# The first load of queries and keys as one of 120 rows and one of 8

## The chip, the core and the metric

The kernel runs on one core of one Trainium2 chip. The metric is the device time of one execution in microseconds (us); the kernel's time is the median of several runs. A core has TensorE (PE; its weight loads are shown apart as PEld), VectorE (DVE), ScalarE (ACT), GpSimd (POOL) and SyncE (SP), each with its own instruction queue, and 16 DMA engines. SPq and ACTq in the rows are the parts of SyncE and ScalarE that issue transfers.

## What is computed

Attention with decay (no softmax) over 8 batches, 8 heads, 576 positions and 64 numbers per head, then a mixture of 8 experts that skips some tokens:

```python
scores = scale * np.matmul(q, k.transpose(0, 1, 3, 2))
Dmat = np.where(rel >= 0, gamma[:, None, None] ** rel[None, :, :], 0.0)
attn = np.matmul(scores * Dmat[None], v)
x = attn.transpose(0, 2, 1, 3).reshape(4608, 512)
do_compute = x @ w_skip > 0
e_idx = np.argmax(x[do_compute] @ w_gate, axis=1)
# for the tokens of expert e: y = gate_w * (relu(xc @ w1[e]) @ w2[e]); out = xc + y; the others: out = x
```

## The kernel before

The 4608 tokens are 36 tiles of 128. The first stage is the attention: for each tile g, SyncE loads a buffer `u` of four sections of 128 rows (partitions) in two halves. The first half (sections 0 and 1) holds queries and keys, 128 rows of 4 KB; the second (sections 2 and 3) holds values and keys in another layout. The second stage, from about 150 us, gathers the tokens of each expert and does the expert products with weights `w`. There are five `u` buffers, so that a load waits until the tile five before it has been used.

At the start the kernel issues, in this order: the decay table `tab_sb` on ScalarE's queue; on SyncE's queue the loads (0, 0), (1, 0), (0, 2), (2, 0), (1, 2), a growth table `gt_sb`, (3, 0), (2, 2), (3, 2), where (g, s) is tile g from section s on; and the router's weights `wg_sb`. Tile 4 and the later ones follow.

While the first load is under way, TensorE runs nine products on a cleared tile (`keep_up`, line 117), and a few more between the first tiles. What it does for tile g afterwards:

- `scores(g)` (line 572, into `psc` and `psq`) needs the first half. Each pair of products reads rows 0 to 63 and rows 64 to 127 of `u` in turn.
- `decay(g)`: VectorE multiplies the scores by masks (lines 587 and 590; the far part also by `dq_sb`, which VectorE makes of the decay table, line 545), and ScalarE copies the rest (line 594) back into `u`.
- `keys(g)` and `rows_of(g)`: GpSimd scales the keys `kn` (line 602) and the values `vs` (line 624) of the second half.
- `state(g)` (line 638), `second(g)` (line 663) and `values(g)` (line 687) are products that need those, and VectorE writes the tile's result (line 699).

The order on each engine comes from a scheduling layer that follows the program's order and the dependences. It gives the transfers of SyncE and ScalarE eight semaphores in rotation: a transfer waits until the one eight places before it has landed.

Of the kernel before, what the change touches and what calls it, by code (L numbers as in the profile page):

```python
# [11 lines left out]
F32 = mybir.dt.float32  # L12
# [10 lines left out]
NTOK, DM, NE, DF = B * S, H * D, 8, 1024  # L23
P = 128
# [3 lines left out]
NPR = H // 2  # L28
# [19 lines left out]
UBUFS = 5  # L48
# [2 lines left out]
AHEAD = 5  # L51
LEAD = 3
GLATE = 4
GROUPS = (8, 8, 8, 4, 4, 4)
KONE = 2
QD = 32
# [32 lines left out]
def kernel(  # L89
# [9 lines left out]
    nc = tc.nc  # L99
# [23 lines left out]
    trank = const.tile([P, NT], F32, tag="trank", name="trank")  # L123
    exs = [const.tile([P, max(GROUPS), NE + 1], F32, tag=f"ex{i}", name=f"ex{i}") for i in range(2)]
    ident = const.tile([P, P], F32, tag="ident", name="ident")
# [19 lines left out]

    cp = ps_m[:, SIDE : SIDE + max(GROUPS) * NCMP].rearrange("p (t k) -> p t k", k=NCMP)
    iota8 = const.tile([P, NE], F32, tag="iota8", name="iota8")
# [68 lines left out]

    starts = np.cumsum((0,) + GROUPS).tolist()

    def tile_numbers(t0, n):
        nc.vector.tensor_copy(cp[:, :n, 0], tidx[:, t0 : t0 + n])  # L220

    def route_b(ps, first, late, pin, n, t0, ex, mb):
# [17 lines left out]
        if first:  # L240
            nc.vector.tensor_copy(cp[:, :, 1], pidx[:, : max(GROUPS)])
            tile_numbers(t0, n)
# [21 lines left out]
        if t0 + n < NT:  # L264
            tile_numbers(t0 + n, GROUPS[starts.index(t0 + n)])

# [226 lines left out]
    with ExitStack() as actx:  # L493
        ac = actx.enter_context(tc.tile_pool(name="ac", bufs=1))
        ap = actx.enter_context(tc.tile_pool(name="ap", bufs=2))
# [14 lines left out]

        u_t = {}

        def load_half(g, s, after=None):
            if s == 0:
                u_t[g] = ap.tile([P, 4, NPR, P], F32, tag="u", name=f"u_{g}", bufs=UBUFS)
            n = 1 if s and g % NQ == HALF else 2
            half = nc.sync.dma_start(
                u_t[g][:, s : s + n].rearrange("p s a i -> p (s a i)"),
                qkv[g, s // 2, :, : n * DM],
            )  # L520
            if after is not None:
                tc.add_manual_dep(
                    half.ins,
                    after.name,
                    mybir.DependencyInfo(mybir.DependencyClass.Sync, mybir.DependencyReason.DATA),
                    reason="the second half begins behind a block of products",
                )

        def last_product():
            return next(i for i in reversed(nc.cur_bb.bb.instructions) if i.engine == mybir.EngineType.PE)  # L530

        nc.scalar.dma_start(tab_sb, tab)
        for g, s in ((0, 0), (1, 0), (0, 2), (2, 0), (1, 2), (3, 0), (2, 2), (3, 2)):
            load_half(g, s)
            if (g, s) == (1, 2):
                nc.sync.dma_start(gt_sb[:, 0], gtab.rearrange("p (a q) -> p a q", a=NPR))
# [94 lines left out]
        def state(g):  # L631

            i = g % NQ
            if i == HALF:
                return
            for a in range(NPR):
                for j in range(2):
                    nc.tensor.matmul(
                        ps_s[halves[j], i % 2, a, :],
                        kn_t[g][:, a, j * D : (j + 1) * D],  # L640
                        u_t[g][:, 2, a, j * D : (j + 1) * D],
                        start=i == 0 and a == 0,
                        stop=a == NPR - 1,
                        skip_group_check=True,
                    )
                yield
            if i == HALF - 1:
                st_t[g + 1] = ap.tile([P, NPR, D], F32, tag="sv", name=f"sv_{g}", bufs=1)
                nc.scalar.copy(st_t[g + 1], ps_s[:, 1])
                return  # L650
            to = joint(g + 2)
            for j in range(2):
                nc.scalar.copy(to[halves[j], j], ps_s[halves[j], i % 2])
# [19 lines left out]
        def in_turn(*products):  # L673

            products = list(products)
            while products:
                products = [p for p in products if next(p, p) is not p]
# [3 lines left out]
        def values(g):  # L681

            pxt = px_t[g]
            q = first(g)
            for a in range(NPR):
                for j in range(2):
                    nc.tensor.matmul(  # L687
                        pxt[halves[j], a, q],
                        vs_t[g][:, j, a, :],
                        u_t[g][:, j, a, q],  # L690
                        start=False,
                        stop=a == NPR - 1,
                        skip_group_check=True,
                    )
                yield
            b, o = divmod(g, NB)
            if o == 0:
                xt_t[b] = ap.tile([P, NPR, NB * P], F32, tag="xt", name=f"xt_{b}")
            nc.vector.tensor_tensor(xt_t[b][:, :, o * P : (o + 1) * P], pxt, gt_sb[:, g % NQ // 2], ALU.mult)
# [64 lines left out]
        def weights():  # L764
# [7 lines left out]
            while held and (held[0] < KFRONT or "first" in marks):  # L772
# [3 lines left out]
                tc.keep_in_program_order(nc.scalar.copy(hi, t))  # L776
                behind = ranked[-1] if len(ranked) == len(GROUPS) - 1 else None
                for m in range(2):
# [78 lines left out]
        for g in range(NT):  # L857
# [5 lines left out]
            in_turn(*products)  # L863
            if g == GLATE:
                load_half(g + UAHEAD - 1, 0, last_product())
            if g and g + UAHEAD - 1 < NT:
                load_half(g + UAHEAD - 1, 2, last_product())
# [17 lines left out]
            in_turn(state(g), *([values(last)] if last >= 0 else []))  # L885
            if g + 1 != GLATE and g + UAHEAD < NT:
                load_half(g + UAHEAD, 0)
# [4 lines left out]
        g = NT  # L892
# [521 lines left out]
```

## Time and profile before

| | us |
|---|---|
| median of 3 runs | 390.61 |
| lowest and highest run | 386.76, 394.09 |
| the profiled execution: its time | 390.34 |
| the profiled execution: its span | 388.6 |
| TensorE busy | 367.6 |
| VectorE busy | 276.0 |
| ScalarE busy | 181.7 |
| GpSimd busy | 152.5 |

The span is the time from the first to the last instruction of the profiled execution; its own time holds 1.7 us more. Busy times overlap between engines. A row of a timeline gives the start, the duration, the engine, the source line, the operation with the tile that it writes and those that it reads, how many instructions were merged, and in brackets how long the engine had been idle before and what ended that.

### The profile page before, as it was taken

What the parts mean: (1) busy time and instruction counts of PE and PEld (TensorE: products, weight loads), DVE (VectorE), ACT (ScalarE), POOL (GpSimd) and SP (SyncE); (2) the same over time, 40 slices, a digit from 0 to 9 for tenths busy, and PEclk for the clock granted to TensorE, in tenths of its full rate; (3) what the DMA queues carried; (4) which work ended last, traced back from release to release, by engine and by line L of the source; (5) the groups of instructions that cost most, each with busy time, mean ns of one, the idle gap of its engine ahead of it and who ended that gap; (6) DMA issues with size and microseconds to landing.
All of it is one profiled execution on the core that took longest, in us unless ns stands there. A gap on an engine that the chain in (4) does not pass through costs nothing. (4 is left out here: it accounts for less than half of the span.)

```text
span 388.6 us, 12328 instructions
## 1 busy us (share of the span) xinstructions
PE 367.6 (95%) x4886; PEld 334.5 (86%) x4886; DVE 276.0 (71%) x615; ACT 181.7 (47%) x369; POOL 152.5 (39%) x211
## 2 busy tenths in 40 slices
PE   7899998989999898999999999999999999999991
PEld 3678877777887776888899999999999999999991
DVE  3576677578579794877856767867878768687762
ACT  2464555355544576117445455445545545555311
POOL 5885855555475389260136000420322322002032
PEclk9999999999999999999999999999999999999997
DMA  8989997989999988257899768978899898776511
GB/s 305 404 281 375 394 351 270 347 299 341 320 359 331 313 319 260 63 128 252 261 317 262 264 212 276 327 228 303 275 278 329 249 336 313 233 253 228 142 68 61
DMA packets 49573, 106.15 MB, mean 273 GB/s; under 512 B 6102, under 2 KB 21206, under 8 KB 49511
## 3 DMA queue, kind: packets, MB, share of 16 engines
q1 hardware_dynamic: 40951, 85.81, 65.2%
q0 software_dynamic: 3232, 9.99, 7.9%
q10 hardware_dynamic: 5328, 9.52, 6.5%
q8 instruction: 40, 0.66, 0.7%
q14 instruction: 22, 0.18, 0.1%
HBM read 83.51 MB, written 22.28 MB: 272 GB/s over the span
## 5 line engine op out<-in xcount | busy, mean ns | idle before, releaser
L171 DVE TENSOR_TENSOR wlo_w<-w,whi_w 128x1024 fp32r<-128x1024 f32 x59 | 72.0, 1223 | 37.8 <-ACT whi_w L170 35.4
L170 ACT CAST whi_w<-w 128x1024 fp32r<-128x1024 f32 x59 | 61.7, 1050 | 33.1 <-PE py L465 32.4
L465 PE MATMUL py<-hlo,whi_w 128*128 128x336 f32 (+6 forms) x224 | 67.8, 303 | 0.0
L465 PE MATMUL ph<-xhi,wlo_w 128*128 128x336 f32 (+6 forms) x224 | 67.6, 302 | 0.0
L465 PE MATMUL ph<-xlo,whi_w 128*128 128x336 f32 (+6 forms) x224 | 67.5, 302 | 0.0
L465 PE MATMUL ph<-xhi,whi_w 128*128 128x336 f32 (+6 forms) x224 | 67.5, 301 | 0.0
L465 PE MATMUL py<-hhi,wlo_w 128*128 128x336 f32 (+6 forms) x224 | 67.5, 301 | 0.0
L465 PE MATMUL py<-hhi,whi_w 128*128 128x336 f32 (+6 forms) x224 | 67.4, 301 | 0.0
L1035 POOL DMA_INDIRECT out<-rs,sidx x17 | 21.2, 1245 | 84.0 <-DVE rs L1034 82.8
L624 POOL TENSOR_TENSOR vs<-u,tab_sb 64x256 f32<-64x256 f32 x72 | 46.7, 649 | 9.9 <-DMA u<-qkv 2.7
L602 POOL TENSOR_TENSOR kn<-u,tab_sb 128x512 f32<-128x512 f32 x32 | 33.8, 1057 | 42.5 <-DMA u<-qkv 18.9
L687 PE MATMUL pxt<-u,vs 128*64 128x128 f32 (+1 forms) x576 | 47.8, 269 | 1.6 <-issue 1.6
L473 ACT ACTIVATE hhi<-ph 128x336 fp32r<-128x336 f32 (+8 forms) x61 | 25.8, 423 | 45.3 <-PE ph L465 45.0
L590 DVE TENSOR_TENSOR u<-psc,tab_sb 64x256 f32<-64x256 f32 x72 | 30.3, 420 | 23.4 <-PE pxt L663 7.7
L594 ACT COPY u<-psc 64x256 f32<-64x256 f32 x64 | 23.4, 366 | 48.7 <-DVE u L590 45.6
L465 PEld LDWEIGHTS ph<-xhi,whi_w 128*128 128x128 f32 x224 | 42.3, 189 | 0.1
L465 PEld LDWEIGHTS py<-hlo,whi_w 128*128 128x128 f32 x224 | 42.2, 188 | 0.2 <-DVE hlo L474 0.2
L465 PEld LDWEIGHTS ph<-xlo,whi_w 128*128 128x128 f32 x224 | 42.3, 189 | 0.1
L465 PEld LDWEIGHTS py<-hhi,whi_w 128*128 128x128 f32 x224 | 42.3, 189 | 0.0
L465 PEld LDWEIGHTS ph<-xhi,wlo_w 128*128 128x128 f32 x224 | 42.3, 189 | 0.0
L465 PEld LDWEIGHTS py<-hhi,wlo_w 128*128 128x128 f32 x224 | 42.3, 189 | 0.0
L572 PE MATMUL psc<-u 64*64 64x128 f32 (+1 forms) x576 | 39.1, 272 | 2.3 <-DMA u<-qkv 2.1
(213 smaller groups left out, 780.7 us busy)
## 6 DMA issues: line engine op xcount, KB each, us to landing
u<-qkv SPq DMA_DIRECT2D x68, 512.0 KB, 6.6
w<-w SPq DMA_DIRECT2D x64, 512.0 KB, 5.5
out<-xn ACTq DMA_DIRECT2D x36, 256.0 KB, 5.8
hop<-xg SPq DMA_DIRECT2D x12, 256.0 KB, 5.2
xh<-hop SPq DMA_DIRECT2D x48, 64.0 KB, 4.9
hopy<-yp SPq DMA_DIRECT2D x24, 128.0 KB, 3.4
yr<-hopy SPq DMA_DIRECT2D x6, 512.0 KB
u<-qkv SPq DMA_DIRECT2D x4, 256.0 KB
```

The costliest lines, as they stand in the source:

```text
L170: nc.scalar.copy(hi, t)
L171: nc.vector.tensor_tensor(lo, t, hi.bitcast(F32), ALU.subtract)
L465: nc.tensor.matmul(ps, x, y, start=first and n == 0, stop=last and n == 3 * len(terms) - 1)
L473: nc.scalar.activation(hi, ph, AF.Relu)
L572: nc.tensor.matmul(psc_t[g][c][halves[1 - j ^ c], a, : q.stop - q.start], u[halves[j], 1 - j, a, c * D : (c + 1) * D], u[halves[j], j, a, ...
L590: nc.vector.tensor_tensor(u_t[g][h, j, :, :D], near[h, :, :D], mt_sb[h].unsqueeze(1).broadcast_to([D, NPR, D]), ALU.mult)
L594: nc.scalar.copy(u_t[g][h, j, :, D:], near[h, :, D:])
L602: nc.gpsimd.tensor_tensor(kn_t[g].rearrange("p a (j i) -> p a j i", j=2), u_t[g][:, 3].rearrange("p a (j i) -> p a j i", j=2), tt_sb[:, k ...
L624: nc.gpsimd.tensor_tensor(vs_t[g][h, j], u_t[g][h, 2, :, j * D : (j + 1) * D], tt_sb[h, TV + g % NQ // 2, :].unsqueeze(2).broadcast_to([D, ...
L687: nc.tensor.matmul(pxt[halves[j], a, q], vs_t[g][:, j, a, :], u_t[g][:, j, a, q], start=False, stop=a == NPR - 1, skip_group_check=True,)
L1035: done = nc.gpsimd.indirect_dma_start(out=out, out_offset=bass.IndirectOffsetOnAxis(ap=idx, axis=0), in_=rs[:n], in_offset=None, bounds_ch ...
```

## The change

The tile's buffer is opened by a function of its own, and the first load, (0, 0), is issued as two: rows 0 to 119 and rows 120 to 127. Both are on SyncE's queue, ahead of (1, 0).

```diff
+LANES = 120
...
+        def open_tile(g):
+            u_t[g] = ap.tile([P, 4, NPR, P], F32, tag="u", name=f"u_{g}", bufs=UBUFS)
+
         def load_half(g, s, after=None):
             if s == 0:
-                u_t[g] = ap.tile([P, 4, NPR, P], F32, tag="u", name=f"u_{g}", bufs=UBUFS)
+                open_tile(g)
...
+        open_tile(0)
         nc.scalar.dma_start(tab_sb, tab)
-        for g, s in ((0, 0), (1, 0), (0, 2), (2, 0), (1, 2), (3, 0), (2, 2), (3, 2)):
+        for rows in (slice(0, LANES), slice(LANES, P)):
+            nc.sync.dma_start(u_t[0][rows, 0:2].rearrange("p s a i -> p (s a i)"), qkv[0, 0, rows, : 2 * DM])
+        for g, s in ((1, 0), (0, 2), (2, 0), (1, 2), (3, 0), (2, 2), (3, 2)):
             load_half(g, s)
```

SyncE's queue at the start, before. The first number in a name is the tile, the last is the scheduler's; `DMAHW0` to `DMAHW7` are the eight semaphores, and `DMAHW0` belongs to the decay table on ScalarE's queue:

```order
L517 DMA u_0_149<-qkv 128x1024
L517 DMA u_1_151<-qkv 128x1024
L517 DMA u_0_149<-qkv 128x1024
L517 DMA u_2_154<-qkv 128x1024
L517 DMA u_1_151<-qkv 128x1024
L536 DMA gt_sb_145<-gtab 128x512
L517 DMA u_3_158<-qkv 128x1024
L517 DMA u_2_154<-qkv 128x1024 [waits DMAHW0_49]
L517 DMA u_3_158<-qkv 128x1024 [waits DMAHW1_49]
L537 DMA wg_sb_147<-wg 128x128 [waits DMAHW2_49]
```

The same queue after the change:

```order
L539 DMA u_0_148<-qkv 120x1024
L539 DMA u_0_148<-qkv 8x1024
L521 DMA u_1_152<-qkv 128x1024
L521 DMA u_0_148<-qkv 128x1024
L521 DMA u_2_155<-qkv 128x1024
L521 DMA u_1_152<-qkv 128x1024
L543 DMA gt_sb_145<-gtab 128x512
L521 DMA u_3_159<-qkv 128x1024 [waits DMAHW0_49]
L521 DMA u_2_155<-qkv 128x1024 [waits DMAHW1_49]
L521 DMA u_3_159<-qkv 128x1024 [waits DMAHW2_49]
L544 DMA wg_sb_147<-wg 128x128 [waits DMAHW3_49]
```

One transfer more stands at the front, so each later one takes the next semaphore: the first half of tile 3, which waited for nothing, now waits for the decay table, the second half of tile 2 for the large part of the first load, and the second half of tile 3 for the small part.

GpSimd's queue at the first tiles, before (`pk` is a small buffer of the second stage):

```order
L602 TENSOR_TENSOR kn_0_199<-u_0_149,tab_sb_146 128x512
L624 TENSOR_TENSOR vs_0_193<-u_0_149,tab_sb_146 64x256 x2
L602 TENSOR_TENSOR kn_1_203<-u_1_151,tab_sb_146 128x512
L624 TENSOR_TENSOR vs_1_196<-u_1_151,tab_sb_146 64x256 x2
L1286 MEMSET pk_131 128x6
L602 TENSOR_TENSOR kn_2_231<-u_2_154,tab_sb_146 128x512
```

The same queue after the change:

```order
L609 TENSOR_TENSOR kn_0_200<-u_0_148,tab_sb_146 128x512
L631 TENSOR_TENSOR vs_0_194<-u_0_148,tab_sb_146 64x256 x2
L1293 MEMSET pk_131 128x6
L609 TENSOR_TENSOR kn_1_204<-u_1_152,tab_sb_146 128x512
L631 TENSOR_TENSOR vs_1_197<-u_1_152,tab_sb_146 64x256 x2
L609 TENSOR_TENSOR kn_2_232<-u_2_155,tab_sb_146 128x512
```

The fill of `pk` has moved ahead of tile 1's keys. On TensorE, VectorE and ScalarE the instructions stand as before; TensorE's first score product now waits for the large part of the first load, and the second one, which reads rows 64 to 127, for the small part.

## Rows read from the trace of the kernel before

**Rows 1.** The page: busy time by engine, and the 40 slices.

```profile
PE 367.6 (95%) x4886; PEld 334.5 (86%) x4886; DVE 276.0 (71%) x615; ACT 181.7 (47%) x369; POOL 152.5 (39%) x211
...
PE   7899998989999898999999999999999999999991
...
DMA  8989997989999988257899768978899898776511
```

**Rows 2.** Windows: stretch, its length, busy time by engine, PEclk, DMA share, GB/s.

```profile
0.00:1.80 1.80, 0.52 (x2) 0.25 (x3) 0.27 (x1) 0.54 (x1) 1.13 (x8) 1.00 0.00 0
1.80:3.90 2.10, 2.10 (x7) 0.72 (x6) 0.00 (x0) 0.94 (x2) 2.00 (x20) 1.00 0.94 282
3.90:5.50 1.60, 1.40 (x4) 0.22 (x2) 0.00 (x0) 0.00 (x0) 0.46 (x2) 1.00 1.06 413
5.50:8.30 2.80, 2.66 (x66) 1.80 (x66) 1.69 (x4) 0.61 (x2) 0.01 (x1) 1.00 1.02 408
8.30:15.00 6.70, 5.29 (x153) 4.11 (x146) 4.72 (x10) 2.95 (x9) 5.94 (x8) 1.00 1.03 404
15.00:135.00 120.00, 112.60 (x2750) 93.42 (x2754) 86.56 (x233) 61.48 (x151) 73.26 (x104) 1.00 0.93 334
```

**Rows 3.** Waits of SyncE's queue, 8 to 135 us: total, times, longest.

```profile
SPq L517 <- PE pxt L687: 46.8, 27, 3.0
SPq L517 <- PE pxt L663: 34.9, 26, 2.9
SPq L517 <- DMA u<-qkv: 5.0, 3, 3.2
```

**Rows 4.** Timeline of SyncE's issues at the start.

```profile
0.83 2.95 SPq L517 DMA_DIRECT2D u<-qkv  x5
...
1.27 0.90 SPq L517 DMA_DIRECT2D u<-qkv  x2
...
4.31 0.49 SPq L517 DMA_DIRECT2D u<-qkv  x1
5.69 0.81 SPq L517 DMA_DIRECT2D u<-qkv  x2
...
6.85 0.33 SPq L537 DMA_DIRECT2D wg_sb<-wg  x1
```

**Rows 5.** Timeline of TensorE, 0 to 10 us.

```profile
1.28 4.02 PE L117 MATMUL ps_m<-mc 128*128 128x512 bf16 x9 [1.28 <-DVE mc L111]
5.55 0.33 PE L572 MATMUL psc<-u 64*64 64x128 f32 x2 [0.26 <-DMA u<-qkv]
...
8.45 0.39 PE L117 MATMUL ps_m<-mc 128*128 128x512 bf16 x1
9.40 0.69 PE L638 MATMUL ps_s<-u,kn 128*64 128x64 f32 x16 [0.56 <-POOL kn L602]
```

**Rows 6.** DMA issues of the whole span: count, KB each, median us from issue to landing.

```profile
u<-qkv SPq DMA_DIRECT2D x68, 512.0 KB, 6.6
...
hopy_r<-yq SPq DMA_DIRECT2D x12, 64.0 KB, 1.8
...
tab_sb<-tab ACTq DMA_DIRECT2D x1, 80.0 KB
wg_sb<-wg SPq DMA_DIRECT2D x1, 64.0 KB
```

**Rows 7.** Timeline of VectorE, 5 to 10 us.

```profile
5.70 0.42 DVE L545 TENSOR_TENSOR dq_sb<-tab_sb 128x256 f32<-128x256 f32 x1 [4.48 <-DMA tab_sb<-tab]
6.70 0.43 DVE L590 TENSOR_TENSOR u<-psc,tab_sb 64x256 f32<-64x256 f32 x1 [0.57 <-PE psc L572]
...
9.03 0.42 DVE L587 TENSOR_TENSOR sq<-psq,dq_sb 128x256 f32<-128x256 f32 x1
```

**Rows 8.** Timeline of GpSimd, 7 to 16 us.

```profile
8.29 1.06 POOL L602 TENSOR_TENSOR kn<-u,tab_sb 128x512 f32<-128x512 f32 x1 [3.89 <-DMA u<-qkv]
...
10.81 1.06 POOL L602 TENSOR_TENSOR kn<-u,tab_sb 128x512 f32<-128x512 f32 x1
...
13.52 0.10 POOL L1286 MEMSET pk<- 128x6 f32 x1
```

**Rows 9.** Issues of the loads, 0 to 8 us: ns of one, min/median/max.

```profile
L517 SPq DMA_DIRECT2D u<-qkv x8: 328/436/788, 0.8 to 6.1; - x8
```

**Rows 10.** Issues of the six tiny transfers of the second stage, in the same form.

```profile
L398 SPq DMA_DIRECT2D pk<-both x6: 756/842/1120, 167.8 to 174.8; - x6
```

## The prediction

> **What bounds the kernel now.** I read the page's busy times and slices first, then the windows of the start, then what each engine did in the first 15 us. TensorE is busy for 95% of the span and the attention stage fills the slices up to about 135 us with DMA digits of 8 and 9 [rows 1]. The reader is to see in the windows that two limits follow each other [rows 2]. From 3.9 to 15 us the 16 DMA engines are full (shares 1.02 to 1.06, 404 to 413 GB/s), so the start is paced by loads. From 15 to 135 us TensorE is busy for 112.60 of 120 us. There SyncE, which issues the loads, waits 46.8 + 34.9 = 81.7 us for products and only 5.0 us for earlier loads [rows 3]: the loads follow the products. So the change acts in a load-bound stretch, and the question is how much of a shift the product-bound stretch hands on.
>
> The first load is issued at 0.83 us [rows 4] and TensorE starts on it at 5.55 us, released by that load [rows 5]. Two rows say that this is late for its size. It holds 512.0 KB (524,288 bytes) and the table beside it 80.0 KB (81,920) [rows 6], together 606 KB of 1000 bytes, as below. Up to 3.9 us 282 GB/s x 2.1 us = 592 KB had moved, up to 5.5 us 413 x 1.6 = 661 KB more [rows 2]. The load counts as landed only when twice the bytes ahead of it have moved, so the 16 engines aren't in step: most are already on later loads while at least one still owes rows of the first. In step, the 606 KB would have passed at 3.9 + 14/413 = 3.93 us. To this comes the time from the last byte to the signal. A lone 64 KB transfer lands 1.8 us after its issue [rows 6]; issue to first byte is 1.8 - 0.83 = about 1.0 us here [rows 2, 4], the bytes are 64/408 = 0.16 us, so at most 0.6 us is left. In step the load would release TensorE at about 4.5 us, 1.0 us before it does. That 1.0 us of lateness of one or a few engines is an estimate from these rows; no row names the engine.
>
> **The change part by part.** The load of 128 rows becomes one of 120 and one of 8. A load of 128 rows gives each of 16 engines 8 rows of 4 KB; at 408 GB/s an engine moves 25.5 GB/s, a row costs 0.161 us and 8 rows 1.28 us [rows 2]. 120 rows are 15 times 8: if they stay at 8 rows an engine, one engine is left out and the 8 rows go to others, one row each.
>
> *First tile.* If the engine left out is the late one, the large part lands at 4.5 us and the small one a row later, 4.5 + 0.16 = about 4.7 us, 0.85 us earlier than 5.55. TensorE can't use all of it: its keep-up products run until 1.28 + 4.02 = 5.30 us [rows 5]. So tile 0's scores start 0.25 us earlier. VectorE's mask at 6.70 waits for these scores, and its table product ends at 6.12, so it moves by the same 0.25 [rows 7].
>
> *Next loads.* The late engine has 8 rows less, 1.28 us against 1.0 us of lateness, so it is no longer last; up to eight others have one row more, 0.16 us. Each later load lands 1.0 - 0.16 = about 0.8 us earlier. The one that matters is tile 0's second half: GpSimd idles until 8.29 us for it [rows 8]; this becomes 7.5. TensorE's next products wait for GpSimd at 9.40 after a gap of 0.56 [rows 5]. Before them stand keep-up products that end at 8.84, or 8.59 once all is 0.25 earlier, so these products start at about 8.65: **0.75 us** earlier. VectorE's second far product at 9.03 to 9.45 moves by 0.25 to 9.20 and lets tile 2's scores go at 9.25, the same 0.75 [rows 5, 7].
>
> *Costs.* One more issue on SyncE ahead of all other loads: no 8-row load is in the trace, the nearest rows go from 0.33 us for the 64 KB load [rows 4, 6] to 1.12 us, the longest of six tiny transfers [rows 10]; I take 0.44, the median of the loads, since it is one of them in all but size [rows 9]. The next load is then issued at 1.27 + 0.44 = 1.7 and its first bytes come at 2.7, while the engines have bytes of the first load and the table until about 3.9 [rows 2]. Covered; without that cover it would cost 0.44 us, at most 1.12.
>
> The semaphores rotate over eight, so every load stands one place later (the listing of the change). Tile 3's first half, issued at 4.31 without a wait, now waits for the table, which releases the next issue at 5.69 and VectorE at 5.70 [rows 4, 7]; behind it on SyncE stand tile 2's and 3's second halves, the router's weights and tile 4. Of what is issued before it (82 + 5 x 524 + 262 = 2964 KB), 592 + 661 + 0.2 x 408 = 1335 KB have moved by 5.7; the rest lasts 4.0 us and the first bytes need 1.0. Covered with 3 us to spare; uncovered it would be 1.4 us. On GpSimd a fill of 0.10 us goes ahead of tile 1's keys, which start with no idle time before them [rows 8]: up to 0.1 us there, and as much less at 13.52. No compute instruction is added; TensorE's second product, one copy and one mask wait for the small part too.
>
> *Sum.* From -0.25 us (tile 0's start alone) to -0.85 us, taken at -0.75. All engines behind it shift together, TensorE has few gaps later, and nothing is tied to the clock on the wall, so it reaches the end: the profiled run goes from 390.34 to 389.6 us (span 388.6 to 387.85). That run lies 0.3 us under the median of 390.61, so the median goes to **389.9 us**.
>
> [...]
>
> **The rivals.** *Nothing arrives at the front (the late engine is kept).* The lateness may sit on one of the 15, or pass to whichever engine is last. For it: no row names the engine. Against: nothing but the excess of bytes, which fits one late engine as well as two. Price: nothing if the late engine gets no further row, 0.16 us if it does: 390.6 to 390.8. [...]
>
> *Shift lost later.* The loads gain 0.8 us, but some wait after 15 us takes it back, for instance the 5.0 us of waits for loads [rows 3]. Against: 81.7 us of waits the other way. 390.6.
>
> *Too few engines (slower).* 120 rows might not be spread over 15. On n engines the large part costs 120/n rows each. With the extra row, this passes 8 rows and the 1.0 us of lateness when (120/n + 1 - 8) x 0.161 > 1.0, from n = 9 downward. On 8 engines later loads land 8 x 0.161 - 1.0 = 0.3 us later: 390.9. On one engine 120 x 0.161 = 19.3 us: first load at 1.85 + 19.3 + 0.6 = 21.8 instead of 5.55, **406.8 us**. Over 2% only for n = 1. For it: no transfer of 120 rows is in the trace. [...]
>
> **How the numbers follow.** Forecast 0.55; late engine kept 0.25; lost later 0.12; too few engines 0.08, of it 0.02 for one engine. All but that last lie between 389.7 and 390.9, far closer together than the three times of before, 386.76 to 394.09, which lie 1.9% apart. A change of under 2% can't be told from none here. So the range is set by the scatter of a median: from 389.9, about 3.5 us each way, 386.4 to 393.6. Faster by over 2% would take a mechanism that I don't see: 0.02. Slower: 0.02 for one engine and 0.01 for scatter: 0.03. Within 2%: 0.95.
>
> **What would show it.** In the changed kernel's profile: tile 0's scores right behind the keep-up products, at 5.3; GpSimd's first keys near 7.5; tile 0's state products near 8.65; SyncE's wait for the table before tile 3; the DMA share from 5.5 to 15 still about 1.0. If scores start at 5.5 or later and keys at 8.3, the late engine was kept. If keys are early and the attention stage ends as late as before, the shift was lost. A first load that lands after 7 us means too few engines. I'd be wrong about the size if the lateness isn't a matter of one engine.

## The result and the profile after

| | median (us) | lowest, highest | runs |
|---|---|---|---|
| before | 390.06 | 386.75, 394.09 | 21 |
| after | 391.83 | 387.5, 396.54 | 21 |

The ratio after to before is 1.0051, 95% interval 1.0026 to 1.0076: the changed kernel is slower by 1.0 to 3.0 us, where the forecast was 0.75 us faster. Two further sets of runs of the same changed kernel, below, give 1.0002 [0.9962, 1.0042] and 1.0036 [1.0002, 1.0071]. The second set alone is not told from no change. The three intervals have the stretch from 1.0026 to 1.0042 in common, about 1.0 to 1.6 us.

Some executions, among them the profiled ones of the changed kernel (396.54 us) and of the kernel with 128 rows of 64 bytes (396.07 us), were disturbed ones that the ratios leave out, so the rows below are of the changed kernel in its third set, profiled at 389.8 us of span. In the second set tile 0's keys and state products start at the same times.

First the windows of the start (columns as in [rows 2]):

```profile
1.80:3.90 2.10, 2.10 (x7) 0.73 (x6) 0.00 (x0) 0.92 (x2) 2.00 (x20) 1.00 0.89 250
3.90:5.50 1.60, 1.40 (x4) 0.21 (x2) 0.43 (x1) 0.00 (x0) 0.45 (x2) 1.00 0.89 192
5.50:8.30 2.80, 2.28 (x50) 1.43 (x54) 1.16 (x3) 0.37 (x1) 0.00 (x0) 1.00 1.01 404
8.30:15.00 6.70, 4.76 (x167) 4.33 (x163) 4.80 (x10) 3.26 (x9) 5.31 (x8) 1.00 1.03 403
15.00:135.00 120.00, 111.68 (x2717) 91.84 (x2709) 84.67 (x229) 58.99 (x146) 71.33 (x102) 1.00 0.93 329
```

From 5.5 us on the rate is that of before again (404 and 403 GB/s against 408 and 404). The loss is small from 1.8 to 3.9 us (250 against 282) and large from 3.9 to 5.5: 192 GB/s against 413, while the DMA engines are nearly as busy (0.89 against 1.06). The DMA view of the whole first 15 us says it in 40 slices of 0.375 us, before:

```profile
GB/s 0 0 0 0 33 197 257 379 237 292 438 410 440 355 426 437 371 404 371 448 415 382 481 344 382 464 404 393 459 393 393 459 382 382 470 339 406 381 426 361
DMA packets 1702, 5.10 MB, mean 340 GB/s; under 512 B 182, under 2 KB 430, under 8 KB 1701
```

and after:

```profile
GB/s 0 0 0 0 3 190 145 314 315 272 256 208 186 197 262 339 437 404 415 404 415 437 404 393 437 404 366 415 399 410 410 426 404 393 426 404 448 377 344 381
DMA packets 1564, 4.67 MB, mean 311 GB/s; under 512 B 173, under 2 KB 396, under 8 KB 1563
```

From 3.75 to 5.6 us the rate is 186 to 262 GB/s where before it stood at 355 or more, and the lost bytes aren't made up later: 0.43 MB fewer have moved by 15 us, which at 408 GB/s is 1.05 us. What the engines do meanwhile is in the DMA view of 3.9 to 5.5 us by queue (packets, MB, share of 16 engines; q1 is SyncE's queue). Before:

```profile
q1 hardware_dynamic: 180, 0.64, 101.8%
```

and after:

```profile
q1 hardware_dynamic: 97, 0.31, 88.9%
```

A share of 100% is 16 x 1.6 = 25.6 us of engine time. Before, a MB takes 1.018 x 25.6 / 0.64 = 40.7 us of it; after, 0.889 x 25.6 / 0.31 = 73.4 us. So the engines are mostly busy, and each byte takes 1.8 times as long. This figure, **engine time per MB**, is used below.

The trace also holds each packet's own time, and a row of 4096 bytes is one packet (before, 157 packets of that size start from 3.9 to 5.5 us, which are the 0.64 MB). From 3.9 to 5.5 us the median row takes 0.159 us before and 0.291 us after (0.308 and 0.300 in the first and second set); from 5.5 to 15 us it takes 0.159 and 0.162. The rows themselves are slow, and only while the 120-row load is under way.

TensorE, the rows that answer to [rows 5]:

```profile
1.27 4.02 PE L118 MATMUL ps_m<-mc 128*128 128x512 bf16 x9 [1.27 <-DVE mc L112]
5.95 0.33 PE L579 MATMUL psc<-u 64*64 64x128 f32 x2 [0.65 <-DMA u<-qkv]
...
10.04 0.34 PE L645 MATMUL ps_s<-u,kn 128*64 128x64 f32 x4 [1.13 <-POOL kn L609]
```

Tile 0's scores start at 5.95 (before 5.55) and its state products at 10.04 (before 9.40). GpSimd, for [rows 8]:

```profile
8.93 1.06 POOL L609 TENSOR_TENSOR kn<-u,tab_sb 128x512 f32<-128x512 f32 x1 [4.54 <-DMA u<-qkv]
...
11.46 0.09 POOL L1293 MEMSET pk<- 128x6 f32 x1
11.52 1.05 POOL L609 TENSOR_TENSOR kn<-u,tab_sb 128x512 f32<-128x512 f32 x1
```

Tile 0's keys wait for its second half until 8.93 (before 8.29). SyncE, for [rows 4]:

```profile
0.83 0.82 SPq L539 DMA_DIRECT2D u<-qkv  x2
1.69 1.89 SPq L521 DMA_DIRECT2D u<-qkv  x4
3.62 1.03 SPq L543 DMA_DIRECT2D gt_sb<-gtab  x1
5.00 1.73 SPq L521 DMA_DIRECT2D u<-qkv  x3
7.49 0.33 SPq L544 DMA_DIRECT2D wg_sb<-wg  x1
```

and VectorE, for [rows 7]:

```profile
5.01 0.43 DVE L552 TENSOR_TENSOR dq_sb<-tab_sb 128x256 f32<-128x256 f32 x1 [3.79 <-DMA tab_sb<-tab]
7.09 0.43 DVE L597 TENSOR_TENSOR u<-psc,tab_sb 64x256 f32<-64x256 f32 x1 [1.65 <-PE psc L579]
...
9.42 0.42 DVE L594 TENSOR_TENSOR sq<-psq,dq_sb 128x256 f32<-128x256 f32 x1
```

Tile 3's first half and the table's reader go together at 5.00 and 5.01: the forecast's new wait is there. It is short.

### The profile page after: what moved, and what is told of

Same layout as the page of the kernel before. It is cut to its first block, busy times and chain, and to the rows that moved or that the text cites. A ratio compares the mean times of both kernels' runs of the same rounds, so it can differ in the third digit from the quotient of the medians.

```text
span 394.8 us, 12330 instructions
## 1 busy us (share of the span) xinstructions
PE 369.6 (94%) x4886; PEld 336.2 (85%) x4886; DVE 276.7 (70%) x615; ACT 181.9 (46%) x369; POOL 149.4 (38%) x211
## 5 line engine op out<-in xcount | busy, mean ns | idle before, releaser
L609 POOL TENSOR_TENSOR kn<-u,tab_sb 128x512 f32<-128x512 f32 x32 | 34.4, 1075 | 51.4 <-DMA u<-qkv 35.8
L1042 POOL DMA_INDIRECT out<-rs,sidx x17 | 19.8, 1163 | 85.0 <-DVE rs L1041 83.8
L694 PE MATMUL pxt<-u,vs 128*64 128x128 f32 (+1 forms) x576 | 48.9, 273 | 1.1 <-issue 1.1
L631 POOL TENSOR_TENSOR vs<-u,tab_sb 64x256 f32<-64x256 f32 x72 | 44.9, 624 | 8.6 <-DMA u<-qkv 1.6
```

Source lines behind the costliest of these rows:

```text
L609: nc.gpsimd.tensor_tensor(kn_t[g].rearrange("p a (j i) -> p a j i", j=2), u_t[g][:, 3].rearrange("p a (j i) -> p a j i", j=2), tt_sb[:, k ...
L631: nc.gpsimd.tensor_tensor(vs_t[g][h, j], u_t[g][h, 2, :, j * D : (j + 1) * D], tt_sb[h, TV + g % NQ // 2, :].unsqueeze(2).broadcast_to([D, ...
L694: nc.tensor.matmul(pxt[halves[j], a, q], vs_t[g][:, j, a, :], u_t[g][:, j, a, q], start=False, stop=a == NPR - 1, skip_group_check=True,)
L1042: done = nc.gpsimd.indirect_dma_start(out=out, out_offset=bass.IndirectOffsetOnAxis(ap=idx, axis=0), in_=rs[:n], in_offset=None, bounds_ch ...
```

## The experiments

The comments behind `#` in the diffs are this text's. The tables give: the ratio to the kernel before, run on the same chip; the start of tile 0's scores on TensorE, of its keys on GpSimd; MB moved by 15 us; engine time per MB on SyncE's queue from 3.9 to 5.5 us. Before has 5.55, 8.29, 5.10 and 40.7; the changed kernel in its first profile 5.93, 9.39, 4.60 and 92.5 (0.29 MB, 104.8%).

### The same kernels again

No edit: the kernel before under another name, and the changed kernel twice.

> The kernel before once more, unchanged: a second profile of its start, and how far two sets of runs of one kernel lie apart. All theories: ratio 0.997 to 1.003. If the start of the first profile is typical, the transfers have moved 1200 to 1300 KB by 5.5 us and 5000 to 5150 KB by 15 us and tile 0's keys start at 8.2 to 8.5 us; the first profile's lateness (tile 0's scores at 5.55 with only half of the moved bytes ahead of them) is a property of one engine if it stands here again, and of that one execution if scores start right behind the keep-up products.

> The changed kernel once more, for its ratio and a second profile. Theory A (rows of a 120-row load move at half pace because its 15 engines get other rows than the 16 of a 128-row load and get in each other's way): tile 0's scores start at 5.7 to 6.1 us (before: 5.55), tile 0's keys at 9.2 to 9.5 us (before: 8.29), and from 1.8 to 5.5 us the transfers move clearly less than the 1253 KB of before, about 800 KB. Theory B (one transfer more: its issue and the rotation of the semaphores cost): the transfers move about as many bytes as before, and later issues are late instead. Both: ratio 1.003 to 1.008.

> The changed kernel a third time, beside the three others on one chip. All theories: keys at 8.9 to 9.4 us, 4550 to 4650 KB by 15 us, ratio 1.001 to 1.007; if the kernels with an extra transfer show the same ratio, the extra transfer is the larger part of the cost, and if they lie at 1.000, the 120 rows are.

| | ratio [95%] | scores | keys | MB | us per MB |
|---|---|---|---|---|---|
| before, a copy | 1.0007 [0.9968, 1.0046] | 5.39 | 8.12 | 5.07 | 38.9 |
| changed, second set | 1.0002 [0.9962, 1.0042] | 5.98 | 8.93 | 4.61 | 78.6 |
| changed, third set | 1.0036 [1.0002, 1.0071] | 5.95 | 8.93 | 4.67 | 73.4 |

A copy scatters by 0.17 us in the start of the keys and 0.03 MB; the changed kernel is 0.64 us or more and 0.4 MB away from both, in each of three profiles. The start tells the kernels apart better than the whole time does.

### How the first load is cut

Rows 64 + 64, then 112 + 16 (the changed kernel with another number):

```diff
-LANES = 120
+LANES = 64    # in the other kernel 112
```

Columns: two transfers as in the changed kernel, but each of 128 rows and half the columns:

```diff
-        for rows in (slice(0, LANES), slice(LANES, P)):
-            nc.sync.dma_start(u_t[0][rows, 0:2].rearrange("p s a i -> p (s a i)"), qkv[0, 0, rows, : 2 * DM])
+        for s in range(2):
+            nc.sync.dma_start(u_t[0][:, s].rearrange("p a i -> p (a i)"), qkv[0, 0, :, s * DM : (s + 1) * DM])
```

Four tiles: the first halves of tiles 0 to 3 all cut, by rows (120 + 8) in one kernel and by columns in the other, with the same number of transfers, order and semaphores:

```diff
-        for g, s in ((1, 0), (0, 2), (2, 0), (1, 2), (3, 0), (2, 2), (3, 2)):
-            load_half(g, s)
+        for g, s in ((0, 0), (1, 0), (0, 2), (2, 0), (1, 2), (3, 0), (2, 2), (3, 2)):
+            if s == 0:
+                open_tile(g)
+                for rows in (slice(0, LANES), slice(LANES, P)):
+                    nc.sync.dma_start(u_t[g][rows, 0:2].rearrange("p s a i -> p (s a i)"), qkv[g, 0, rows, : 2 * DM])
+            else:
+                load_half(g, s)
```

> The first load as 64 and 64 rows: each part can use 16 engines with 4 rows each, so no engine is left out and no engine has a row more than another. Theory A (what counts is which rows an engine has beside the others, not their number): each part reaches only half of the 128 rows, the pace stays at half, scores at 5.7 to 6.3 us, keys at 9.0 to 9.6 us, ratio 1.002 to 1.008. Theory C (the load is slow because 15 engines and an uneven share are used): scores at 5.3 to 5.6 us, keys at 8.2 to 8.5, ratio 0.998 to 1.001. Theory B (one transfer more): ratio 1.003 to 1.008, with the bytes up to 5.5 us as before.

> The first load as 112 and 16 rows: both can use 16 engines (7 rows and 1 row each), but 7 rows an engine are again other rows than in a load of 128. Theory A: below the full pace, 800 to 1150 KB moved by 5.5 us against 1253 and 4600 to 4900 KB by 15 us against 5102; keys at 8.6 to 9.3 us; ratio 1.001 to 1.005. Theory C (15 engines and the uneven share are the cost): as before, 1250 KB and 5100 KB, keys at 8.2 to 8.5, ratio 0.998 to 1.001.

> The first load as two of 128 rows and half the columns each (2 KB a row): the number of transfers, their place in the queue and the rotation of the semaphores are those of the changed kernel, and each part covers all 128 rows. Theory A: the full pace is back, scores at 5.3 to 5.6 us, keys at 8.2 to 8.5 us, ratio 0.998 to 1.001. Theory B (one transfer more): keys as late as in the changed kernel or the queue late behind them, ratio 1.003 to 1.008.

> The first halves of tiles 0 to 3 all go out as 120 and 8 rows. Theory A: each of the four loads costs 8 rows at about 0.30 instead of 0.16 us, 1.1 us; two of them stand ahead of tile 0's keys, which start at 10.2 to 10.8 us, and at 15 us the transfers are 3 to 4.5 us behind those of before; ratio 1.007 to 1.013 (1.006 if the products catch part of it up). Theory B: three issues more of 0.44 us, covered by what is queued: keys at 9.2 to 9.8 us, ratio 1.003 to 1.009 with no lower rate of the transfers. If the cost is that of the very first load alone (a start effect): as the changed kernel, keys at 9.4, ratio 1.003 to 1.008.

> The control to the four tiles in 120 and 8 rows: the first halves of tiles 0 to 3 go out as two of 128 rows and half the columns each, so that the number of transfers, their order and their semaphores are the same and only the rows differ. Theory A: full pace, 4700 to 5100 KB moved by 15 us (four tiles in 120 and 8 rows: 3429), keys at 8.3 to 8.9 us, ratio 0.999 to 1.004. Theory B (transfers and semaphores more): as the four tiles in 120 and 8 rows, keys near 10.0 us, ratio 1.013 to 1.022.

| | ratio [95%] | scores | keys | MB | us per MB |
|---|---|---|---|---|---|
| 64 + 64 | 1.0024 [0.9984, 1.0065] | 5.23 | 8.72 | 4.78 | 55.0 |
| 112 + 16 | 1.0015 [0.9965, 1.0065] | 5.22 | 9.43 | 4.63 | 59.5 |
| columns | 1.0008 [0.9975, 1.0042] | 4.99 | 8.73 | 4.74 | 42.4 |
| four tiles by rows | 1.0174 [1.0126, 1.0222] | 5.77 | 10.02 | 3.43 | 73.3 |
| four tiles by columns | 1.0040 [1.0007, 1.0074] | 5.22 | 8.76 | 4.84 | 46.7 |

The pair of four tiles decides for the rows. Windows of the one by rows:

```profile
3.90:5.50 1.60, 1.29 (x4) 0.21 (x2) 0.42 (x1) 0.00 (x0) 0.56 (x3) 1.00 1.03 228
5.50:8.30 2.80, 1.67 (x38) 1.00 (x38) 1.27 (x3) 0.40 (x2) 0.00 (x0) 1.00 1.00 237
8.30:15.00 6.70, 3.34 (x102) 3.00 (x106) 3.24 (x8) 2.16 (x7) 3.62 (x5) 1.00 1.05 281
```

and of the one by columns:

```profile
3.90:5.50 1.60, 1.60 (x11) 0.49 (x13) 0.43 (x1) 0.00 (x0) 0.46 (x2) 1.00 0.99 338
5.50:8.30 2.80, 2.53 (x66) 1.77 (x62) 1.27 (x3) 0.73 (x2) 0.00 (x0) 1.00 1.03 368
8.30:15.00 6.70, 5.07 (x148) 4.11 (x146) 4.27 (x9) 2.93 (x8) 5.35 (x8) 1.00 1.04 401
```

In both the engines are full (last column but one), and in the first they move 228 to 281 GB/s all the way, as long as such loads are in the queue. The ratios lie 0.0134 apart, 5.2 us, or 1.3 us for each of the four loads; by their two intervals, 2.9 to 7.5 us, or 0.7 to 1.9 each. The bytes moved by 15 us lie 1.41 MB apart, 3.5 us at 408 GB/s, or 0.9 us a load. In the kernel by rows the median row takes 0.280 us still from 5.5 to 15 us, in the one by columns a row of the same 4 KB 0.159. So the rows of the 120-row loads move at a little over half the pace here, whichever tile they belong to, and the extra transfers and semaphores that both kernels share don't explain it.

112 + 16 and 64 + 64 lie between (59.5 and 55.0 us per MB). That each of their parts uses 16 engines is the author's estimate and was not shown. Their rows are of two kinds from 3.9 to 5.5 us: a quarter take 0.265 us or more and 0.290 us or more, another quarter 0.162 us or less. They also have a transfer behind the first load, which turned out to matter by itself (next), so how their loss divides isn't told apart.

### A transfer behind the first load

The column kernel had full pace (42.4 us per MB) and still late keys (8.73). So the first load was left whole, and a transfer that the computation doesn't need was added, into a buffer that is filled again much later: 8 rows of 4 KB directly behind the first load, the same at the end of the first loads, one row of 64 bytes directly behind the first load, and 128 rows of 64 bytes there. The lines of the first; the others differ in the place or the size:

```diff
         for g, s in ((0, 0), (1, 0), (0, 2), (2, 0), (1, 2), (3, 0), (2, 2), (3, 2)):
             load_half(g, s)
+            if (g, s) == (0, 0):
+                nc.sync.dma_start(xg0[:8, 0:2].rearrange("p k c -> p (k c)"), qkv[0, 0, P - 8 :, :])
...
+            if (g, s) == (3, 2):    # at the end: the same line under this condition
...
+                nc.sync.dma_start(xg0[:1, 0, :16], qkv[0, 0, :1, :16])    # 64 bytes
...
+                nc.sync.dma_start(xg0[:, 0, :16], qkv[0, 0, :, :16])      # 128 rows of 64 bytes
```

> The first load stays one of 128 rows, and a transfer of 8 rows (the last 8 rows once more, into the buffer of the second stage's first gather, where nobody reads them) follows it: the issue, its place, the rotation of the semaphores and an extra row on eight engines are those of the changed kernel. Theory A: 32 KB more, 0.1 to 0.2 us; keys at 8.3 to 8.6 us, 4900 to 5100 KB moved by 15 us, ratio 0.998 to 1.002. Theory B (one transfer more): keys at 9 us or later or a queue that falls behind, ratio 1.003 to 1.006.

> The extra transfer of 8 rows stands at the end of the first loads, ahead of the router's weights, and not behind the first load. Theory D (an added transfer costs where it stands at the front, because the loads behind it reach the engines late): the start is that of before, tile 0's keys at 8.0 to 8.4 us, 5000 to 5130 KB by 15 us, ratio 0.998 to 1.002. Theory B (it costs wherever it stands, by one semaphore and one issue more): keys as before but 4700 to 4850 KB by 15 us, ratio 1.002 to 1.005.

> The extra transfer behind the first load is one row of 64 bytes instead of 8 rows of 4 KB. If the 8 rows cost by their bytes and by falling on few of the 128 rows (theory E): no cost is left, keys at 8.0 to 8.4 us, 5000 to 5130 KB by 15 us, ratio 0.998 to 1.002. Theory D (any transfer there costs): keys at 8.7 to 9.2 us, 4700 to 4800 KB, ratio 1.001 to 1.005.

> The extra transfer behind the first load is 128 rows of 64 bytes: all 16 engines get 8 short rows. Theory E (8 rows cost by falling on few of the 128 rows): no cost is left, keys at 8.0 to 8.5 us, 4950 to 5130 KB by 15 us, ratio 0.998 to 1.002. Theory D (any transfer there costs, as an issue of 128 rows the more so): keys at 8.7 to 9.3 us, 4600 to 4800 KB, ratio 1.001 to 1.006.

| | ratio [95%] | scores | keys | MB | us per MB |
|---|---|---|---|---|---|
| 8 rows behind the first load | 1.0034 [0.9996, 1.0072] | 4.71 | 9.07 | 4.75 | 56.1 |
| 8 rows at the end | 1.0023 [0.9980, 1.0066] | 5.41 | 8.10 | 4.98 | 43.9 |
| 64 bytes behind the first load | 1.0014 [0.9977, 1.0051] | 5.06 | 9.22 | 4.81 | 51.4 |
| 128 rows of 64 bytes there | 1.0000 [0.9950, 1.0050] | 4.91 | 9.01 | 4.75 | 60.4 |

Even 64 bytes make tile 0's keys 0.9 to 1.1 us later than in the two profiles of before, though the scores start sooner:

```profile
9.22 1.06 POOL L604 TENSOR_TENSOR kn<-u,tab_sb 128x512 f32<-128x512 f32 x1 [4.83 <-DMA u<-qkv]
```

The DMA view of 3.9 to 5.5 us with the 64 bytes, SyncE's queue:

```profile
q1 hardware_dynamic: 111, 0.41, 82.4%
```

Here the queue leaves the engines idle for 18% of the stretch (with the 120 rows 11% in the set shown, nothing in the two others). And the rows aren't slow: the median is 0.159 to 0.165 us in all three kernels with a transfer in this place. The higher time per MB comes from a few packets of 0.5 to 1.7 us. The trace also has the times at which a load's semaphore is counted up: for a load of 128 rows 16 times (before, the first load from 3.86 to 5.51 us), as many as there are DMA engines, and the counts of one load follow those of the load before it by 1.3 us, about the time of eight rows. A count is therefore read below as one engine landing its part; this is an estimate, since the trace names no engine. With the 64 bytes, twelve engines land load (1, 0) at 5.36 to 5.95 us and four at 7.69 to 7.77. So, by this reading, a few engines stall, and the load waits for them.

Four more kernels, each run once with the kernel before beside it, ask which part of it costs. All loads behind the first, and nothing added, wait for a short count on GpSimd:

```diff
-            load_half(g, s)
+            load_half(g, s, None if (g, s) == (0, 0) else counted_up)
```

The 64-byte transfer on ScalarE's queue behind the decay table, on SyncE's queue behind load (1, 0), and on SyncE's queue ahead of the first load:

```diff
         nc.scalar.dma_start(tab_sb, tab)
+        nc.scalar.dma_start(xg0[:1, 0, :16], qkv[0, 0, :1, :16])
...
+            if (g, s) == (1, 0):
+                nc.sync.dma_start(xg0[:1, 0, :16], qkv[0, 0, :1, :16])
...
+        nc.sync.dma_start(xg0[:1, 0, :16], qkv[0, 0, :1, :16])
         for g, s in ((0, 0), (1, 0), (0, 2), (2, 0), (1, 2), (3, 0), (2, 2), (3, 2)):
```

> No added transfer: the first load goes out whole, and all loads of SyncE behind it wait until GpSimd has ended a short count, at about 1.5 us, so that the load of tile 1 is issued at about 1.6 us in place of 1.3. A normal start is tile 0's keys at 8.0 to 8.4 us and 5000 to 5130 KB moved by 15 us, a delayed one 8.7 to 9.3 us and 4700 to 4850 KB. If what costs is that the second large load is issued some 0.4 us later: a delayed start. If it is the transfer as such (a place in the queue or in the engines' work): a normal start, or one late by the 0.3 us of the delay itself, keys at 8.3 to 8.6.

> An added transfer of 64 bytes, but on ScalarE's queue, behind the decay table; SyncE's queue is as in the kernel before, apart from the semaphores, which stand one place on. If what costs is the time or the place on SyncE's queue: a normal start, keys at 8.0 to 8.4 us and 5000 to 5130 KB by 15 us. If it is one more transfer anywhere in the first 2 us, or the semaphores that stand one place on: a delayed one, keys at 8.7 to 9.3 us and 4700 to 4850 KB.

> The 64-byte transfer on SyncE's queue, one load later: behind the first load of tile 1 and so ahead of tile 0's second half. If what costs is the pause between the first and the second large load: a normal start, keys at 8.0 to 8.5 us and 4950 to 5130 KB by 15 us, since two large loads are under way by then. If any added transfer ahead of tile 0's second half costs: a delayed one, keys at 8.7 to 9.3 us and 4700 to 4850 KB.

> The 64-byte transfer on SyncE's queue ahead of the first load, so that all loads are issued about 0.4 us later and their spacing is that of the kernel before. If only the pause between the first and the second load costs: keys later by those 0.4 us alone, 8.5 to 8.7 us, and the rate from 3.9 us on stays near 400 GB/s. If an added transfer near the front costs as such: keys at 8.9 to 9.5 us, and a stretch between 3.9 and 8.3 us well under 350 GB/s.

| | time, before beside it | scores | keys | MB | us per MB |
|---|---|---|---|---|---|
| later issue, no transfer | 393.64, 392.45 | 5.22 | 7.91 | 4.97 | 48.9 |
| 64 bytes on ScalarE's queue | 393.46, 392.45 | 5.23 | 7.96 | 5.17 | 40.2 |
| 64 bytes behind (1, 0) | 391.14, 392.45 | 5.22 | 8.01 | 5.03 | 41.7 |
| 64 bytes ahead of the first load | 394.68, 392.45 | 5.38 | 8.31 | 5.01 | 41.7 |

The single times scatter by more than what is asked. The keys answer: all four start normally, in the last one no later than its 0.4 us later issue allows. In the first of them load (1, 0) is issued at 1.55 in place of 1.27 [rows 4] (with the 64 bytes in that place at 1.67), and the keys are not late for it. The keys of the four, in order:

```profile
7.91 1.06 POOL L611 TENSOR_TENSOR kn<-u,tab_sb 128x512 f32<-128x512 f32 x1 [3.35 <-DMA u<-qkv]
...
7.96 1.06 POOL L603 TENSOR_TENSOR kn<-u,tab_sb 128x512 f32<-128x512 f32 x1 [3.57 <-DMA u<-qkv]
...
8.01 1.06 POOL L604 TENSOR_TENSOR kn<-u,tab_sb 128x512 f32<-128x512 f32 x1 [3.62 <-DMA u<-qkv]
...
8.31 1.06 POOL L603 TENSOR_TENSOR kn<-u,tab_sb 128x512 f32<-128x512 f32 x1 [3.92 <-DMA u<-qkv]
```

So, in one profile each, neither an issue later by 0.28 us, nor one transfer more, nor the semaphores' shift (the second and third have it too) delays the start. What is left is a transfer in one place, between the first load and (1, 0) on their queue. Why some engines stall for it is open.

### How the changed kernel's loss divides

Both the 120 rows and a transfer in that place are in the changed kernel. Two kernels keep its 120 rows and take the 8 out of that place, to ScalarE's queue behind the decay table, and ahead of the 120:

```diff
-        for rows in (slice(0, LANES), slice(LANES, P)):
-            nc.sync.dma_start(u_t[0][rows, 0:2].rearrange("p s a i -> p (s a i)"), qkv[0, 0, rows, : 2 * DM])
+        for q, rows in ((nc.sync, slice(0, LANES)), (nc.scalar, slice(LANES, P))):
+            q.dma_start(u_t[0][rows, 0:2].rearrange("p s a i -> p (s a i)"), qkv[0, 0, rows, : 2 * DM])
...
+        for rows in (slice(LANES, P), slice(0, LANES)):    # in the other kernel
```

> The changed kernel with its 8 rows on ScalarE's queue, behind the decay table; SyncE's queue holds the 120 rows and then the loads as before. If the changed kernel's loss is two things, the half pace of the 120 rows and a transfer that stands directly behind the first load, only the first is left: scores near 5.9 us, the rate from 3.9 to 5.5 us still low, but keys near 8.4 to 8.7 and 4700 to 4850 KB by 15 us, between the changed kernel's (8.93 and 9.39; 4604 to 4663 KB) and the kernel before. If the half pace alone makes the whole loss: as the changed kernel, keys at 8.9 or later. If the place alone makes it: keys at 8.0 to 8.3 us and 5000 KB or more.

> The changed kernel with its two parts in the other order on SyncE's queue: the 8 rows first, then the 120. No transfer stands between the large part and the load of tile 1, but all is issued some 0.4 us later. If both the half pace and the place count: keys near 8.7 to 9.0, 4600 to 4750 KB by 15 us, as the kernel with the 8 rows on ScalarE's queue and 0.3 to 0.4 us on top. If the half pace alone makes the loss: keys at 9.3 or later, the changed kernel's with 0.3 us on top. If the place alone makes it: keys at 8.3 and 5000 KB, as with a tiny transfer ahead of the first load.

| | ratio [95%] | scores | keys | MB | us per MB |
|---|---|---|---|---|---|
| 8 rows on ScalarE's queue | 1.0013 [0.9985, 1.0041] | 6.55 | 9.07 | 4.62 | 73.1 |
| 8 rows first | 1.0032 [0.9995, 1.0068] | 6.45 | 9.66 | 4.58 | 70.1 |

GpSimd with the 8 rows on ScalarE's queue:

```profile
9.07 1.06 POOL L609 TENSOR_TENSOR kn<-u,tab_sb 128x512 f32<-128x512 f32 x1 [4.68 <-DMA u<-qkv]
```

Bytes and engine time are near the changed kernel's (4.60 to 4.67, and 73 to 79 in its second and third set), and so are the keys of the first (8.93 to 9.39). The median row takes 0.278 and 0.261 us. So the slow rows alone make a loss at the start as large as the changed kernel's, and the place adds nothing that shows. Of the outcomes put down beforehand these are those of the slow rows alone (keys at 8.9 or later, and at 9.3 or later); that both causes add up is not borne out. The scores don't fit: they start about half a microsecond later than the changed kernel's 5.93 to 5.98, and the runs don't say why. The ratios are too coarse to add to this. No timed kernel of the study beats the kernel before.

## Why the prediction was wrong

**The step that failed: the price of a row.** The prediction says "a row costs 0.161 us and 8 rows 1.28 us", and gives the 120 rows the same price. That price was taken from loads of 128 rows. In the 120-row load the median row took 0.291 us, so eight rows on one engine cost an estimated 2.3 us, 1.0 to 1.1 us more; the 73.4 us per MB give the same (0.30 us a row, against 0.167 at before's 40.7). The pair of four tiles gives 0.9 us a load by bytes and 1.3 by time, and the bytes that are missing at 15 us give 1.05 us. These agree with the 1.0 to 1.6 us that the three ratios share. No rival covered this: "too few engines" priced fewer engines at an unchanged row, and a trace with no 120-row load in it gave no bound for the row itself. The costs got a bound from both sides; this term did not. Why the rows are slow stays open.

The spread itself came as forecast; the prediction took it as a condition, and no row of before shows it. The semaphore of the 120 rows is counted up once at 1.42 us, before any byte has moved, and then 15 times from 4.67 to 5.90; that of the 8 rows once at 1.82 and then 8 times from 4.88 to 5.89 (in the changed kernel's first profile 1.43 and 15 times from 4.84 to 5.89, 1.82 and 8 times from 5.29 to 5.91). With a count read as an engine, as above, 15 engines and 8 engines carried them.

**The premise of one late engine held, but its size was that of one profile.** The times at which engines landed their parts, by the counts (us; the changed kernel is its third set):

| | load | 8th of 16 engines | 15th | last |
|---|---|---|---|---|
| before | (0, 0) | 4.26 | 4.54 | 5.51 |
| before | (1, 0) | 5.58 | 5.86 | 6.83 |
| before | (0, 2) | 6.86 | 7.16 | 8.12 |
| changed | (1, 0) | 6.71 | 7.26 | 7.47 |
| changed | (0, 2) | 7.99 | 8.56 | 8.76 |

Before, fifteen engines had landed the first load by 4.54 us, as the prediction worked out for engines in step, and one came 1.0 us behind them, on the next loads too. In the changed kernel the last engine is 0.2 us behind the 15th (0.2 to 0.3 in its other profiles). So the late engine is gone, but the 8th engine of each load lands 1.1 us later. With the measured row, the forecast of tile 0's second half 0.8 us earlier becomes about 0.3 us later; its keys came 0.64 us later, so part of the gain did not come.

The size was chance: in the ten profiles of kernels with a whole first load the last engine lands it 0.08 to 0.97 us behind the 15th (0.65 in the copy of before), and 0.97 is the profile that the prediction read. The 0.08 is the kernel with 8 rows behind the first load, where nothing is taken from any engine. Its load has landed at 4.67, and its scores start at 4.71:

```profile
3.38 1.30 PE L117 MATMUL ps_m<-mc 128*128 128x512 bf16 x4
4.71 0.33 PE L574 MATMUL psc<-u 64*64 64x128 f32 x2
```

The keep-up products end at 4.68 there, against 5.30 before, so the prediction's 5.30 was no fixed bound for the scores either. Whether the engine that was left out of the 120 rows is the late one, the trace doesn't say: it doesn't name the engines.

**Tile 0's scores** were forecast at 5.3 and came at 5.93 to 5.98, released by the load; **keys** at 7.5, came at 8.93 to 9.39; **state products** at 8.65, came at 10.04 to 10.51. The chain from the second half through GpSimd to TensorE held: in the third set keys and state products move by the same 0.64 us (8.29 to 8.93, 9.40 to 10.04). They move the other way, because the second half lands later.

**The costs.** The extra issue took what was forecast: (1, 0) at 1.69, forecast 1.7. That it is covered holds for a delay of 0.28 us (the later issue without a transfer leaves keys at 7.91). As a transfer in that place it would not have been covered behind a whole first load (keys 9.07), a cost that the prediction did not have; in the changed kernel it adds nothing that shows. The wait for the table is there and covered: released at 5.00, with the DMA share at 1.01 and 1.03 behind it. The fill of `pk` takes 0.09 us ahead of tile 1's keys, which start without a gap behind it.

**The shift to the end.** Single profiles don't show it: whole times of one kernel lie some 7 us apart. The timed dose does: four such loads move the whole time by 5.2 us (2.9 to 7.5) between the pair, whose bytes by 15 us are 3.5 us apart. What the load-bound start loses, the end loses too; that it loses exactly as much is not shown.

**Two transfers in place of one** are not what slowed the rows: by columns, with as many transfers in the same places, the engine time is 42.4 us per MB (40.7 before), by 120 and 8 rows 73.4 to 92.5. Which rows an engine carries, no run here shows.

## What to carry to other kernels

Price a transfer of a new shape as unknown, from below and from above, even if the byte count is the same: here the same 512 KB cost about 1 us more (0.9 to 1.3 by the four-tile pair) when the rows went from 128 to 120 + 8. To tell a slow transfer from a waiting one, divide the engines' busy time by the bytes moved in the stretch; a busy share near 1 says nothing about pace (1.06 at 413 GB/s before, 1.03 at 228 with four tiles by rows). Then look at the median packet: slow rows (0.29 us against 0.159) and a few long packets (0.5 to 1.7 us) among normal rows raise that figure alike. Before a lateness read from one profile goes into a sum, read it in a second one. Repeat a suspected small cost several times in one kernel, beside a control with the same number of transfers: four times the cost was clear where one was at the edge of the scatter.

## What was unexpected of the hardware

While a load of 120 rows is under way, a row of 4 KB takes 0.26 to 0.31 us, with loads of 128 rows 0.159; in engine time, 70 us per MB or more against the 39 to 41 of the two profiles of before. A transfer of 64 bytes directly behind the first load makes the second half of tile 0 land 0.9 us later and leaves 0.26 to 0.29 MB unmoved by 15 us (4.81 against 5.07 and 5.10); on the other queue, one load later or ahead of the first load it does not. By the counts of its semaphore it holds up a few engines only: four of 16 land load (1, 0) 1.7 us behind the others. Each of these rests on one profile, but the 8 rows and the 128 rows of 64 bytes in the same place show the same (keys 9.07 and 9.01). Its effect on the whole time is not told from none (1.0014, 1.0034 and 1.0000, all with 1 in their intervals), and its cause stays open.
